# A gated long-convolution and linear-attention kernel rebuilt: FFT turns as matmuls, kernel tables made ahead, streams interleaved

## The chip, the cores and the metric

The kernel runs on one core of one Trainium2 chip. The metric is device time of one execution in microseconds (us); lower is better. Several executions are timed and the median is quoted.

## The reference

The output mixes two branches per row with a gate g. Branch `a` is a state-space convolution: for each of 512 channels a kernel K of 2048 taps is built from 128 complex exponentials, and u (2048 rows, 512 channels) is convolved with it through an FFT of length 4096. Branch `b` is linear attention with 32 heads of 16. The reference, cut to what matters:

```python
def reference(A_u, ..., B_wqkv, B_w_phi, B_wo, gate_w):
    # branch a
    logdA = dt * A                                         # complex, (512, 128)
    P = jnp.exp(logdA[:, :, None] * l[None, None, :])      # (512, 128, 2048)
    K = jnp.einsum("dn,dnl,dn->dl", Cc, P, dB).real        # (512, 2048)
    Kf, Uf = rfft(pad(K)), rfft(pad(u.T))                  # length 4096
    y = irfft(Uf * Kf)[:L].T + u * Dskip
    # branch b
    q, k, v = split(x @ wqkv)
    phi_q = concat(softmax(q w_phi), softmax(-q w_phi))    # phi_k alike
    o = (phi_q @ sum_s phi_k v) / (phi_q . sum_s phi_k + 1e-6)
    b = o @ wo
    # both
    g = sigmoid((x * gate_w).sum(-1))
    return g * y + (1 - g) * b                             # x = u
```

## The kernel before

Matmuls leave their results in PSUM, from where VectorE or ScalarE copies them out; such a copy is called an eviction here. The kernel runs phase after phase: loads and keys, queries and attention output, the FFT of u, and then four quarters of 128 channels, each with kernel generation, FFT of K, product, inverse FFT and output. An FFT step mixes rows within a partition block, and the next step needs another axis on the partitions. Before makes that turn by a trip through DRAM: SU for u, UHd for u's spectrum (written whole, read back by quarter), SK for K, SZ for the product.

```python
def kgen_chunk(nc, kp, c, cc, E_L, E_R, nE_R, psA, psK, wk, kst_sc):   # 32 channels
    ...                                                  # phase table of the left factor
    y = wk.tile([128, 32, 32], F32, name="k_y")
    nc.scalar.activation(out=y[:], in_=ps[:], func=ACT.Identity, bias=MAGIC)
    nc.vector.scalar_tensor_tensor(out=nf[:], in0=y[:], scalar=MAGIC, in1=ps[:], op0=ALU.subtract, op1=ALU.subtract)
    nc.scalar.activation(out=anf[:], in_=nf[:], func=ACT.Abs)
    nc.scalar.activation(out=msinL[:], in_=nf[:], func=ACT.Sin, scale=TWO_PI_S)
    nc.scalar.activation(out=cosL[:], in_=anf[:], func=ACT.Sin, scale=-TWO_PI_S, bias=HALF_PI)
    nc.vector.tensor_tensor(out=Lre[:], in0=E_L[:, dl0:dl0 + 32, :], in1=cosL[:], op=ALU.mult)
    nc.vector.tensor_tensor(out=mLim[:], in0=E_L[:, dl0:dl0 + 32, :], in1=msinL[:], op=ALU.mult)
    ...                                                  # right factor: Rre, Rim
    for pair in range(16):
        nc.tensor.matmul(o, lhsT=Rre[:, 2 * pair:2 * pair + 2, :], rhs=Lre[:, 2 * pair:2 * pair + 2, :], start=True, stop=False)
        nc.tensor.matmul(o, lhsT=Rim[:, 2 * pair:2 * pair + 2, :], rhs=mLim[:, 2 * pair:2 * pair + 2, :], start=False, stop=True)

def fft_stage_a(nc, fc, sc, kst_sc, SK, fp):
    ...                                                  # first step of K into Kt
    for ri in range(2):
        eng = nc.sync if ri == 0 else nc.scalar
        eng.dma_start(out=SK[ri, :, :, d0:d0 + 128].rearrange("q f d -> f q d"), in_=Kt[ri][:])
    st.MQ = fp.mq.tile([128, 32, 128], BF16, name="MQK")
    for ri in range(2):
        eng.dma_start(out=st.MQ[64 * ri:64 * ri + 64, :, :], in_=SK[ri, :, :, d0:d0 + 128].rearrange("q (fq f) d -> (q fq) f d", fq=4))

def fft_stage_b(nc, fc, st, Uh, SZ, fp):
    ...                                                  # second step, product: 8 x 6 DVE operations of 512
    for ro in range(2):
        eng.dma_start(out=SZ[ro, :, :, d0:d0 + 128].rearrange("q (fq f) d -> (q fq) f d", fq=4), in_=Zt[64 * ro:64 * ro + 64, :, :])
    for ro in range(2):
        eng.dma_start(out=st.ZT[ro][:], in_=SZ[ro, :, :, d0:d0 + 128].rearrange("q f d -> f q d"))

# full_kernel
BSd, gs = part_b(...)                                    # attention, whole
UHd = u_path_dram(nc, tc, fc, x2d, dram)                 # FFT of u, whole: SU, MQU, UHd
for qtr in range(5):
    ...                                                  # exp tables of the quarter
    for cc in range(4):
        if qtr < 4: kgen_chunk(...)
        if pending is not None:
            if cc == 0: ...; fft_stage_b(nc, fc, pending, Uh, SZ, fp)
            elif cc == 1: fft_stage_c(nc, fc, pending, fp, make_final(128 * pending.sc)); pending = None
    if qtr < 4: pending = fft_stage_a(nc, fc, qtr, kst_sc, SK, fp)
```

The softmax here doesn't subtract the row's maximum and nothing guards it: scores larger than these inputs give would overflow.

## Time and profile before

| | before |
|---|---|
| time, median of 3 runs | 647.84 us (643.49 to 651.64) |
| span of the profiled execution | 644.2 us |
| mean TensorE clock granted | 0.715 |
| instructions | 5205 |

The page cuts the span into 40 equal slices, here of 16.1 us. A digit is the busy share of an engine in that slice in tenths (9 is 90% or more); PE is TensorE, DVE VectorE, ACT ScalarE. PEclk is the TensorE clock in tenths, DMA the busy share of the 16 DMA engines. From the kernel before:

```profile
PE   0197738726755404655464654746536556452442
...
DVE  2399994397765503534725975449835399351932
ACT  0176529929533403568997534975448764441210
...
DMA  9800010400383885853015096160861707817035
...
DMA packets 150171, 61.20 MB, mean 95 GB/s; under 512 B 136704, under 2 KB 148224, under 8 KB 148992
```

Read the columns downwards. The fifteenth is the plainest: DMA 8, and 0 in all three rows above. In the second half, peaks of DMA return every few slices and no compute row holds an 8 or 9 for more than two slices: transfers and computing take turns. And 61.20 MB go in 150,171 packets, most under 512 bytes, while u and the output are 2 MB each. The groups, stages and chain that the argument starts from are in the prediction below.

### The profile page before, as it was taken

The page shows a single profiled execution, that of the slowest core. Times are in us where ns is not written, and L with a number is a line of the kernel's source. Part 1 is how long each engine was busy: PE and PEld are TensorE (multiplying, and loading weights), DVE is VectorE, ACT ScalarE, POOL GpSimd, SP SyncE. Part 2 cuts the span into 40 slices and gives each one's busy share as a digit, 9 for nine tenths or more (in the row PEclk, how much of TensorE's full clock was granted, in tenths as well). Part 3 has the DMA queues.
Part 4 walks back from the last instruction along what each step waited for, and adds up shares of the span by engine and source line. Part 5 has one row for each costly group of instructions (what it writes and reads, how often), then busy time and mean ns, then how long its engine had stood idle before and what let it go on. Part 6 is the DMA issues. An engine that isn't in the chain of part 4 may idle for free.

```text
span 644.2 us, 5205 instructions
## 1 busy us (share of the span) xinstructions
PE 334.6 (52%) x1600; PEld 127.8 (20%) x1600; DVE 384.0 (60%) x821; ACT 334.7 (52%) x477; POOL 49.7 (8%) x83
## 2 busy tenths in 40 slices
PE   0197738726755404655464654746536556452442
PEld 0143313201221101212231221312203121130010
DVE  2399994397765503534725975449835399351932
ACT  0176529929533403568997534975448764441210
POOL 9431000000360000000000000000000000000000
PEclk9999979959985856877676575765757766556565
DMA  9800010400383885853015096160861707817035
GB/s 156 163 1 2 1 11 0 127 4 1 112 249 104 236 228 162 243 247 66 1 44 87 1 184 128 49 98 1 158 137 38 126 0 128 163 37 130 0 66 113
DMA packets 150171, 61.20 MB, mean 95 GB/s; under 512 B 136704, under 2 KB 148224, under 8 KB 148992
## 3 DMA queue, kind: packets, MB, share of 16 engines
q1 hardware_dynamic: 77728, 29.52, 20.6%
q10 hardware_dynamic: 71264, 28.22, 20.4%
q0 software_dynamic: 1152, 3.15, 1.7%
q8 instruction: 12, 0.20, 0.1%
q14 instruction: 15, 0.12, 0.1%
HBM read 30.86 MB, written 26.87 MB: 90 GB/s over the span
## 4 chain that ended last, share of the span: by engine, by line
DMA 32%; DVE 31%; ACT 17%; PE 14%; issue 4%; ACTq 1%; DVEq 0%; SPq 0%
DMA SZ<-Zt 5%; DMA MQK<-SK 4%; DMA SU<-Ut 3%; DMA xT<-in_A_u_dram 3%; DVE Kre L422 3%; DMA UHd<-Uo 2%; DVE ot L744 2%; DMA MQU<-SU 2%; ACT E_R L209 2%; PE ups L674 2%; PE psP L391 2%; DVE phik L517 2%; DVE phik L519 1%; DVE k_y L222 1%; ACT k_anf L224 1%
## 5 line engine op out<-in xcount | busy, mean ns | idle before, releaser
L251 PE MATMUL kps<-k_Lre,k_Rre 128*128 128x64 bf16 x256 | 29.5, 238 | 33.1 <-DVE k_Lre L231 32.9
L676 DVE CAST Uo<-ups 128x512 bf16<-128x512 f32 x32 | 20.8, 687 | 40.9 <-PE ups L674 29.5
L423 ACT CAST Kim<-psQim 128x512 bf16<-128x512 f32 x32 | 18.5, 590 | 43.6 <-PE psQim L419 43.6
L678 ACT CAST Uo<-ups 128x512 bf16<-128x512 f32 x32 | 18.1, 587 | 43.6 <-PE ups L674 32.7
L418 PE MATMUL psQre<-MQK,BDQ_1649 128*128 128x512 bf16 x32 | 19.0, 594 | 32.0 <-DMA MQK<-SK 20.8
L251 PEld LDWEIGHTS <-k_Rre 128*128 128x128 bf16 x256 | 26.7, 128 | 37.9 <-DVE k_Lre L231 20.2
L209 ACT ACTIVATE E_R<-argps 128x1024 bf16<-128x1024 f32 x32 | 32.5, 1056 | 0.7 <-PE argps L206 0.6
L744 DVE SCALAR_TENSOR_TENSOR ot<-psY,gs,bs_in 128x128 bf16<-128x128 f32 x64 | 17.5, 342 | 25.0 <-PE psY L458 22.5
L422 DVE CAST Kre<-psQre 128x512 bf16<-128x512 f32 x32 | 21.8, 680 | 15.5 <-PE psQre L418 15.5
L206 PE MATMUL argps<-selR_110,statER 128*128 128x512 bf16 x64 | 22.4, 436 | 15.6 <-ACT E_L L201 12.7
L252 PE MATMUL kps<-k_mLim,k_Rim 128*128 128x64 bf16 x256 | 28.7, 239 | 2.3 <-DVE k_Rim L247 2.3
L252 PEld LDWEIGHTS <-k_Rim 128*128 128x128 bf16 x256 | 26.6, 128 | 15.7 <-issue 8.7
L232 DVE TENSOR_TENSOR k_mLim<-E_L,k_msinL 128x1024 bf16<-128x1024 bf16 x16 | 11.0, 689 | 31.1 <-ACT k_msinL L226 31.1
L210 DVE TENSOR_SCALAR nE_R<-E_R 128x4096 bf16<-128x4096 bf16 x4 | 4.9, 1227 | 40.0 <-ACT E_R L209 40.0
L419 PE MATMUL psQim<-MQK,BDQ_1650 128*128 128x512 bf16 x32 | 18.8, 589 | 17.3 <-DVE Kre L422 17.3
L627 PE MATMUL bps<-wo_sb,oT 128*128 128x512 bf16 x64 | 20.4, 465 | 12.6 <-ACT bs L629 11.7
L674 PE MATMUL ups<-MQU,BDQ_1649 128*128 128x512 bf16 x32 | 10.8, 462 | 30.1 <-DMA MQU<-SU 28.1
L629 ACT ACTIVATE bs<-bps,omg 128x512 bf16<-128x512 f32 x16 | 11.0, 687 | 23.7 <-DVE bs_1433 L633 4.4
L607 PE MATMUL aexp<-a_pm,Xst 128*128 128x512 bf16 x32 | 13.8, 443 | 17.1 <-DVE a_pm L599 14.7
L220 ACT ACTIVATE k_y<-argps 128x1024 f32<-128x1024 f32 x16 | 16.6, 1037 | 11.2 <-DVE ot L744 9.8
L443 ACT CAST Zt<-psZ 128x512 bf16<-128x512 f32 x16 | 9.4, 585 | 25.1 <-PE psZ L439 25.1
L224 ACT ACTIVATE k_anf<-k_y 128x1024 f32<-128x1024 f32 x16 | 16.8, 1052 | 8.9 <-DVE k_y L222 8.8
(792 smaller groups left out, 998.0 us busy)
## 6 DMA issues: line engine op xcount, KB each, us to landing
UHd<-Uo SPq DMA_DIRECT2D x4, 1024.0 KB, 4.3
UHd<-Uo ACTq DMA_DIRECT2D x4, 1024.0 KB, 4.3
bs_in<-BSd SPq DMA_DIRECT2D x16, 128.0 KB, 2.5
SU<-Ut SPq DMA_DIRECT2D x2, 1024.0 KB, 11.0
SU<-Ut ACTq DMA_DIRECT2D x2, 1024.0 KB, 9.6
MQU<-SU SPq DMA_DIRECT2D x1, 2048.0 KB, 12.7
MQU<-SU ACTq DMA_DIRECT2D x1, 2048.0 KB, 12.7
MQK<-SK SPq DMA_DIRECT2D x4, 512.0 KB, 6.9
```

The costliest lines, as they stand in the source:

```text
L206: nc.tensor.matmul(ps[:, 8 * j:8 * j + 8, :], lhsT=kp.statER[:, G, :], rhs=kp.selR64[:, d0:d0 + 8, :], start=True, stop=True)
L209: nc.scalar.activation(out=E_R[:, dd:dd + 16, :], in_=ps[:], func=ACT.Exp)
L224: nc.scalar.activation(out=anf[:], in_=nf[:], func=ACT.Abs)
L251: nc.tensor.matmul(o, lhsT=Rre[:, 2 * pair:2 * pair + 2, :], rhs=Lre[:, 2 * pair:2 * pair + 2, :], start=True, stop=False)
L252: nc.tensor.matmul(o, lhsT=Rim[:, 2 * pair:2 * pair + 2, :], rhs=mLim[:, 2 * pair:2 * pair + 2, :], start=False, stop=True)
L418: nc.tensor.matmul(psre[:], lhsT=fc.BDQ[0][:], rhs=MQ[:, fs, :], start=True, stop=True)
L419: nc.tensor.matmul(psim[:], lhsT=fc.BDQ[1][:], rhs=MQ[:, fs, :], start=True, stop=True)
L422: nc.vector.tensor_copy(out=Kre[:], in_=psre[:])
L627: nc.tensor.matmul(ps[:], lhsT=oT[:, m, 128 * st:128 * st + 128], rhs=wo_sb[:, m, :], start=(m == 0), stop=(m == 3))
L674: nc.tensor.matmul(ps[:], lhsT=fc.BDQ[ro][:], rhs=MQ[:, fp_, :], start=True, stop=True)
L676: nc.vector.tensor_copy(out=Uo[:, ff, :], in_=ps[:])
L744: nc.vector.scalar_tensor_tensor(out=ot[:, qq, :], in0=ps[:, qq, :], scalar=gs[:, q:q + 1], in1=bs[:, qq, :], op0=ALU.mult, op1=ALU.add)
```

## The change

The intent is to remove the turns, to have fewer and larger vector operations, and to let independent streams fill each other's gaps. Four parts:

1. **Turns of data become matmuls.** The data is the stationary operand (`lhsT`) and the FFT table the moving one, so that the product comes out turned. SU, SK and UHd go; one DRAM turn per quarter (Zd) stays, in halves. (The attention branch's output also still waits in DRAM until its quarter is put together, in `bSd`, as in before.)
2. **Kernel generation.** The left factor is a product of two small polar tables C and D, worked out once. Exponentials and sines of 64 channels are made one piece ahead of their use, with one switch of ScalarE's function table each way.
3. **Attention by blocks** of 256 (keys) and 512 rows (queries); the output projection is folded into `Mw`.
4. **Program order interleaves** the streams.

The diff cut to its core:

```diff
-def kgen_chunk(nc, kp, c, cc, E_L, E_R, nE_R, psA, psK, wk, kst_sc):
-    ...                                    # left phase table per chunk, see above
+def kgen_a(nc, C, D, wk, d0, n):
+    ...
+    for o, (i0, j0), (i1, j1), op in ((0, (0, 0), (1, 1), ALU.add), (1, (0, 1), (1, 0), ALU.subtract)):
+        nc.vector.tensor_tensor(out=A[:, o], in0=Cb(i0), in1=Db(j0), op=ALU.mult)
+        nc.vector.tensor_tensor(out=tmp[:], in0=Cb(i1), in1=Db(j1), op=ALU.mult)
+        nc.vector.tensor_tensor(out=A[:, o], in0=A[:, o], in1=tmp[:], op=op)
+def kgen_chunk(nc, kps, A, R):
+    for e in range(2):
+        for g4 in range(4):
+            for ri in range(2):
+                for dj in range(4):
+                    d = 16 * e + 4 * dj + g4
+                    nc.tensor.matmul(kps[32 * dj:32 * dj + 32, g4, e, :], lhsT=A[:, ri, :, :, d].rearrange("p a b -> p (a b)"),
+                                     rhs=R[:, ri, d, :], start=(ri == 0), stop=(ri == 1), tile_position=(0, 32 * dj), skip_group_check=True)
...
-        eng.dma_start(out=SK[ri, :, :, d0:d0 + 128].rearrange("q f d -> f q d"), in_=Kt[ri][:])
-        eng.dma_start(out=st.MQ[64 * ri:64 * ri + 64, :, :], in_=SK[...])
+def fft_stage_a(nc, fc, ps_pool, lhs, XA_dst, ev):
+    ...
+            nc.tensor.matmul(ps[:, i, :], lhsT=l[0], rhs=rhs, start=True, stop=True)     # data stationary
+    ev(XA_dst, ps[:].rearrange("p g (x d) -> p x d g", d=4))
...
-        for b in range(8): ...             # 6 products and sums of 512, Kre and Kim apart
+        nc.vector.tensor_tensor(out=t12[:], in0=Us, in1=XK[:], op=ALU.mult)
+        nc.vector.tensor_tensor(out=t34[:], in0=Us, in1=XK[:, :, ::-1, :], op=ALU.mult)
+        ...                                # the sums are made in PSUM by the inverse's matmuls
+            nc.sync.dma_start(out=Zd[:, :, rs, :].rearrange("i t r d -> (i t) r d"), in_=Z[:, rs, :])
+            ...
+                    nc.sync.dma_start(out=ZT[p0:p0 + step, :, :], in_=Zd[ri, 32 * th:32 * th + 32, rs, :].rearrange("t r d -> r t d"))
...
-    BSd, gs = part_b(...)
-    UHd = u_path_dram(nc, tc, fc, x2d, dram)
-    for qtr in range(5): ...
+    polar = compute_polar(nc, act, persist, tp, ring, rawd, ld_b, ident)
+    C, D = next(polar)
+    act.begin(TRIG)
+    next(polar, None)
+    ...
+    fold_projection(nc, at, wraw, 512, wT, Wkp, ident, ring, evu)
+    u_path(nc, fc, UD, xau, XU, ring, evu, 2)
+    ...                                    # keys, fold
+    query(0)
+    tabs[1] = kgen_tables(1)
+    Eq[2] = query_exp(nc, act, qp, psA, xT, Wqp, 2)
+    query(1)
+    kgen(0)
+    ...
+    fft(0)
+    for Q in range(1, 4):
+        for h in (2 * Q, 2 * Q + 1):
+            if h + 1 < 8:
+                tabs[h + 1] = kgen_tables(h + 1)
+            kgen(h)
+        fft(Q)
+        finish(Q - 1)
+    finish(3)
```

## The prediction

> **What bounds the kernel now.** I read the page's busy shares first, then the windows by stage, the chain of waits, and the costs by group.
>
> ```profile
> PE 334.6 (52%) x1600; PEld 127.8 (20%) x1600; DVE 384.0 (60%) x821; ACT 334.7 (52%) x477; POOL 49.7 (8%) x83
> ```
>
> No engine is full: the busiest, VectorE (DVE), works 384.0 of 644.2 us. The loss is in the gaps, so I cut the span where the program changes stage (columns: stretch, length, then busy time of PE, PEld, DVE, ACT and POOL, TensorE clock, DMA share, GB/s).
>
> ```profile
> 0.00:83.00 83.00, 43.34 (x364) 23.21 (x365) 60.08 (x164) 33.51 (x62) 32.64 (x59) 1.00 0.37 63
> 83.00:205.00 122.00, 72.96 (x244) 24.55 (x244) 84.50 (x172) 71.14 (x120) 17.11 (x24) 0.81 0.27 78
> 205.00:283.00 78.00, 33.38 (x96) 10.89 (x95) 32.79 (x51) 27.80 (x49) 0.00 (x0) 0.69 0.73 218
> 283.00:341.00 58.00, 32.31 (x206) 14.72 (x207) 24.06 (x33) 52.08 (x59) 0.00 (x0) 0.76 0.25 64
> 341.00:423.00 82.00, 46.38 (x224) 17.75 (x224) 51.39 (x109) 50.82 (x62) 0.00 (x0) 0.63 0.49 90
> ...
> 587.00:645.00 58.00, 19.96 (x40) 4.29 (x40) 28.14 (x76) 7.03 (x12) 0.00 (x0) 0.53 0.37 64
> ```
>
> Loads and attention keys take 0 to 83, queries and attention output 83 to 205, the FFT of u 205 to 283, then four quarters of 128 channels, 82 us apart, and a tail of 58 us. In the FFT of u no compute engine is half busy and DMA has 73%: it goes through DRAM twice. In a repeated quarter DVE works 51 of 82 us. The chain of waits says what the rest is:
>
> ```profile
> DMA 32%; DVE 31%; ACT 17%; PE 14%; issue 4%; ACTq 1%; DVEq 0%; SPq 0%
> ```
>
> A third of the end-setting chain (206 us) is transfers. In its time order the second quarter shows them naked:
>
> ```profile
> 422.82 6.45 DMA MQK<-SK
> ...
> 462.81 9.74 DMA SZ<-Zt
> 472.58 4.29 DMA ZT_3516<-SZ
> ```
>
> With the 2.69 us of SK<-Kt ahead of them, 23 us per quarter. So the bound is **latency**: phases in order, four DRAM turns inside them, TensorE half cold in between.
>
> **What the Trainium skill says.** (1) "TensorE: Matmul & The Clock Gate", Part 1: the array runs at half clock until it has been busy for about 3.4 us. Agrees: the clock is 1.00 up to 83 us and 0.53 in the tail; 64-column matmuls follow each other every 53 ns in the timeline near 304 us, 512-column ones every 216 ns near 37 us and 430 ns near 98 us. (2) "VectorE: DVE Perf Modes", tier table: two-source operations do two bf16 elements a cycle from SBUF and one from PSUM. Agrees: k_mLim, 1024 bf16 elements, 689 ns; the PSUM cast Kre, 512 elements, 680 ns. (3) "TensorEngine Tiling (Array Packing)", Key Properties: small tiles work in parallel, but changing the tiling mode drains the engine. No trace here shows either: the one tiled group of before (the query sums) has its tiles 216 ns apart, one after another. (4) "ScalarE: Activation LUTs", What ACT_TABLE_LOAD costs: 1283 ns for the load. Agrees: every load of the trace takes 1283 ns.
>
> **The change, part by part.** I use five durations of before: DVE two-source bf16, 1024 elements, 0.69 us; DVE with a PSUM or f32 source, 512 elements 0.69 and 1024 elements 1.22 (k_y, 1212 ns); ACT 512 elements 0.59, 1024 elements 1.04; small operations 0.2 to 0.4.
>
> ```profile
> L222 DVE SCALAR_TENSOR_TENSOR k_y<-k_y,argps 128x1024 f32<-128x1024 f32 x16 | 19.4, 1212 | 0.4 <-ACT k_y L220 0.4
> L232 DVE TENSOR_TENSOR k_mLim<-E_L,k_msinL 128x1024 bf16<-128x1024 bf16 x16 | 11.0, 689 | 31.1 <-ACT k_msinL L226 31.1
> L422 DVE CAST Kre<-psQre 128x512 bf16<-128x512 f32 x32 | 21.8, 680 | 15.5 <-PE psQre L418 15.5
> L423 ACT CAST Kim<-psQim 128x512 bf16<-128x512 f32 x32 | 18.5, 590 | 43.6 <-PE psQim L419 43.6
> L209 ACT ACTIVATE E_R<-argps 128x1024 bf16<-128x1024 f32 x32 | 32.5, 1056 | 0.7 <-PE argps L206 0.6
> ```
>
> *Kernel generation.* The left phase table per chunk (k_y, k_anf, k_msinL, k_cosL, E_L on ACT; k_y, k_Lre, k_mLim on DVE) goes; its values come from products of two small tables, C and D. DVE per 32 channels: 6 + 4 two-source operations of 1024 and one negation: 10 x 0.69 + 0.42 = 7.3; sixteen times: 117 us. ACT per 64 channels: 4 exponentials + 4 sines x 1.04 + 2 table loads 2.6 + 3 evictions 3.1 = 14; eight times: 112 us.
>
> *FFT of K, inverse, output.* Turns of data become matmuls with the data stationary; SK is gone, one DRAM turn (Zd, in halves) stays. Per quarter DVE: 8 products x 0.69 + 2 output products x 1.22 = 8 us, where before it had 6 x 8 x 0.42 + 8 x 0.68 + 4 x 0.69 + 16 x 0.34 = 34. ACT: 8 evictions x 1.04 = 8. Four quarters: DVE 34 with two evictions of the last, ACT 31.
>
> *FFT of u.* Both DRAM turns go (SU<-Ut, MQU<-SU, UHd<-Uo, about 50 us of the chain), and the stage becomes 32 evictions, plus 8 of the folded projections: ACT 27 x 1.02 = 28, DVE 13 x 1.22 = 16.
>
> *Attention.* Keys: per 256 rows DVE 2 reductions x 1.22 + 4 x 0.69 = 5.2, ACT 3.0; eight times 42 and 24. Folding 4 and 6. Queries: per 512 rows DVE 8 x 0.69 + 1.5 = 7.0, ACT 8 x 0.6 + 1.5 + 4 x 0.59 = 8.7; four times 28 and 35. The output projection is folded into Mw, so oT with its evictions goes, and the long reciprocals (3.3 us each) go to exp and ln on ACT.
>
> *Set-up.* FFT constants, selectors, masks: DVE 23, ACT 5. Rates and polar tables C, D: DVE 40, ACT 27 (16 f32 passes of 512 and four trigonometric blocks of 1024). Turning x, gates, table loads: ACT 13.
>
> *Sums.* DVE 117 + 34 + 16 + 42 + 4 + 28 + 23 + 40 = 304, against 384. ACT 112 + 31 + 28 + 24 + 6 + 35 + 5 + 27 + 13 = 281, against 335. PE issues about 4,700 matmuls against 1,600, most small. By columns: 448 of 512, 448 of 256, 1,632 of 128, 2,176 of 64 or fewer. At the paces above (216, 108, 54 and 30 ns warm, the last two estimated from the first and from 27 ns between 1-column matmuls near 24 us) that is 97 + 48 + 88 + 65 = 298 us one after another and warm, about 560 cold (430, 215, 107, 53). Parallel tiles would save up to a quarter; I take **340**, my least certain number.
>
> *From sums to a span.* Three engines now have near 300 each, so no stage can be shorter than its busiest engine; I go through the stages. Loads, constants, rates: u is 2 MB in 256-byte pieces; before moved such pieces at 1 MB in about 6.5 us (MQK), so 14 us behind the first loads; DVE has 27 us: 30. Polar tables with turning x, the FFT of u and the folds beside them: ACT 62, DVE 53, with ping-pong between them: 65, to 95. Keys: before, DVE ran them gaplessly at 2.9 us per 128 rows; now 2.6 of work but longer chains: 50, to 145. Fold: 8. Queries with the first two kernel pieces beside them: DVE 57, ACT 63, PE 90 to 110: 85, to 238. Three quarters of kernel and FFT, DVE 37, ACT 36, PE 28 warm and 48 cold in each, sharing two PSUM slots for tables and kernel blocks: 43 each, to 367. Tail of the last quarter: FFT and inverse 17, two DRAM legs at 4 to 6 us partly behind it 7, output 12: about 36. Together **403**.
>
> **The rivals.**
> - *TensorE becomes the bound.* For it: three times the instructions, weights read at strides (the A slices and the turned u), mode changes that drain, a clock that falls in gaps (0.63 in the repeated quarters). Against: 340 of 403 is hidden if the streams do mix. If tiles don't overlap and it stays cold: 480 to 520.
> - *PSUM slots and single buffers replace the DRAM wait.* R, Atmp and KD have one buffer and a kernel block holds one of two slots for two chunks, about 9 of 15 us. If each quarter serializes to 60, the time is 403 + 3 x 17 = 455.
> - *The streams mix perfectly.* DVE at 85% would give 304 / 0.85 = 358. For it: before ran DVE without a gap from 40 to 80 us when its inputs were there.
> - *The removed turns were hidden anyway.* Against: they lie naked on the chain. Only Zd stays, and it has the next quarter's kernel to hide behind, except in the last.
>
> **Range and chances.** The centre is the stage sum, 403; the mixing rival sets the low end, 345, the PSUM and part of the TensorE rival the high end, 475. Even the worst I can build, 520, is 20% below 647.84 us, so "slower" has only what I can't see: faster 0.97, same 0.01, slower 0.02.
>
> **What would show it.** DVE busy 290 to 320 and ACT 265 to 300 confirm the sums; PE busy above 400 or a mean clock below 0.65 makes TensorE the failed term. The DMA share of the chain should fall from 32% to under 12%, most of it in the first 20 us and the last 20. The kernel products of 1024 must take near 0.69 us although one operand is repeated; at 1.22 DVE would gain 96 x 0.53 = 51 us and the time about 45. The repeated quarter should be near 43 us. If PE waits most for PSUM slots to be emptied, the second rival is right.

## The result, and the profile after

| | before | after |
|---|---|---|
| time, median of 4 | 646.13 us (643.49 to 651.64) | 411.48 us (410.56 to 412.68) |
| ratio, with its 95% interval | | 0.6363 (0.6327 to 0.6400) |
| span profiled | 644.2 us | 410.5 us |
| VectorE, ScalarE, TensorE busy | 384.0, 334.7, 334.6 us | 274.2, 257.2, 271.4 us |
| mean clock | 0.715 | 0.763 |
| moved by DMA | 61.20 MB | 21.54 MB |

The output is correct.

The page of the kernel after, the busy line, the slices (now of 10.3 us) and the chain:

```profile
PE 271.4 (66%) x4712; PEld 164.5 (40%) x4712; DVE 274.2 (67%) x470; ACT 257.2 (63%) x335; POOL 7.2 (2%) x19
...
PE   0465100397997877879997999764876778767621
...
DVE  8956667644477847943874379697959695925502
ACT  3589452888565494786549726979695979643000
...
PEclk9985555589699989688999899886588656665555
DMA  9991000000000000000010011255000950045894
...
ACT 34%; PE 28%; DVE 24%; DMA 6%; issue 4%; SPq 2%; DVEq 0%; ACTq 0%
```

DMA has nearly gone from the end-setting chain (6% where before had 32%), and from the fifth slice to the twenty-fifth its row shows 0 or 1. Three engines share the chain, none full. Two holes are left: the fifth to seventh slices, where PE shows 1, 0, 0, and the last three, where ScalarE shows 0.

The windows of the trace after, cut where the program changes stage (same columns as in the prediction):

```profile
0.00:27.00 27.00, 9.36 (x151) 8.52 (x152) 21.25 (x62) 15.90 (x18) 7.18 (x19) 1.00 1.09 186
27.00:76.00 49.00, 7.81 (x68) 6.56 (x67) 33.46 (x63) 28.53 (x37) 0.00 (x0) 0.51 0.10 25
76.00:103.00 27.00, 21.25 (x569) 19.35 (x569) 14.49 (x14) 21.63 (x24) 0.00 (x0) 0.81 0.01 2
103.00:158.00 55.00, 47.12 (x607) 18.92 (x607) 36.33 (x48) 35.28 (x62) 0.00 (x0) 0.91 0.01 2
158.00:170.00 12.00, 7.95 (x106) 3.35 (x106) 10.79 (x26) 4.68 (x11) 0.00 (x0) 0.78 0.00 0
170.00:254.00 84.00, 77.81 (x802) 40.00 (x800) 55.36 (x100) 54.68 (x90) 0.00 (x0) 0.93 0.07 25
254.00:367.00 113.00, 79.32 (x1906) 52.37 (x1905) 88.11 (x146) 90.54 (x92) 0.00 (x0) 0.71 0.33 69
367.00:411.00 44.00, 20.74 (x520) 15.43 (x519) 14.43 (x16) 5.91 (x7) 0.00 (x0) 0.50 0.73 121
```

They are set-up, polar tables, FFT of u, keys, fold, queries with the first kernel pieces, the repeated quarters, and the tail. Between 254 and 367 us VectorE and ScalarE work 78% and 80% of the time; that is where mixing pays. In the tail ScalarE works 5.91 of 44 us.

The first hole, in the timeline (start, length, instruction, in brackets the idle time before it and what ended it), and the second, from the chain's order of time:

```profile
34.39 2.83 PE L381 MATMUL psA<-W,UD 128*64 128x256 bf16 x24
...
40.35 0.99 ACT L70 CAST Wkp<-wps 128x1024 bf16<-128x1024 f32 x1
...
43.69 1.28 ACT L91 ACT_TABLE_LOAD   x1
...
77.15 3.81 PE L381 MATMUL psA<-W,UD 128*64 128x256 bf16 x32 [34.64 <-ACT XAu L70]
```

```profile
386.67 4.49 DMA Zd<-Z
...
394.19 6.79 DMA ZT<-Zd
```

UD, u as it was loaded, was there early: the same operation had done 24 matmuls from 34.39 us on and 8 more at 41.39, which fill the four PSUM slots that it has. Then PE idled 34.6 us, until the first evictions into XAu, which ran only after the polar tables' sines. Order alone is a poor explanation: in the program text the folded key projection stands behind the sines too, and its evictions ran ahead of them (Wkp at 40.35, the sines' table load at 43.69). What sets XAu apart is that the program gives it its memory only where the tables' scratch has been freed. So the wait looks like one for memory; experiment 6 comes back to it. At the end the last quarter's turn lies open: 4.49 us out, 3 us until the loads of ZT had been issued one after the other, 6.79 us until the last landed.

The groups of the after page that answer to the durations used in the prediction (busy us, mean ns of one, then the idle time before them):

```profile
L96 ACT ACTIVATE E<-args 128x1024 bf16<-128x1024 f32 x32 | 31.3, 1034 | 2.9 <-PE args L313 2.9
...
L91 ACT ACT_TABLE_LOAD x20 | 25.7, 1283 | 1.1 <-PEq L917 0.7
L341 DVE TENSOR_TENSOR A<-Ctab,Dtab 128x1024 bf16<-128x1024 bf16 x32 | 21.6, 690 | 6.6 <-PE kps L368 6.6
...
L368 PE MATMUL kps<-R,A 128*32 128x64 bf16 x1024 | 19.8, 234 | 5.1 <-ACT cs L96 3.5
```

The kernel products take 690 ns although one operand is repeated. The 1,024 kernel matmuls last 234 ns each, 240 us if laid end to end, but keep PE busy for 19.8 us: they overlap.

### The profile page after: what moved, and what is told of

Same layout as the page of the kernel before. It is cut to its first block, busy times and chain, and to the rows that moved or that the text cites. A ratio compares the mean times of both kernels' runs of the same rounds, so it can differ in the third digit from the quotient of the medians.

```text
span 410.5 us, 10580 instructions
## 1 busy us (share of the span) xinstructions
PE 271.4 (66%) x4712; PEld 164.5 (40%) x4712; DVE 274.2 (67%) x470; ACT 257.2 (63%) x335; POOL 7.2 (2%) x19
## 2 busy tenths in 40 slices
DMA packets 56317, 21.54 MB, mean 52 GB/s; under 512 B 52048, under 2 KB 54736, under 8 KB 56272
## 4 chain that ended last, share of the span: by engine, by line
ACT 34%; PE 28%; DVE 24%; DMA 6%; issue 4%; SPq 2%; DVEq 0%; ACTq 0%
PE bps L680 6%; ACT E L96 5%; ACT cs L96 4%; ACT L91 3%; PE pk L576 3%; ACT Eq L96 3%; DMA UD<-in_A_u_dram 3%; PE psz L444 3%; ACT XK L70 2%; PE psB L402 2%; DVE vr L591 2%; DVE Eq L676 2%; ACT Ek L96 2%; ACT xT L70 2%; ACT Z L70 2%
## 5 line engine op out<-in xcount | busy, mean ns | idle before, releaser
L444 PE MATMUL psz<-t,TI 64*128 64x128 bf16 x512 | 28.7, 277 | 16.2 <-DVE t L435 12.6
L444 PEld LDWEIGHTS <-TI 64*128 64x128 bf16 x512 | 23.5, 124 | 28.0 <-issue 22.8
L680 PE MATMUL bps<-Mw,Eq 128*128 128x512 bf16 x128 | 33.6, 410 | 1.4 <-DVE Eq L676 1.1
L96 ACT ACTIVATE E<-args 128x1024 bf16<-128x1024 f32 x32 | 31.3, 1034 | 2.9 <-PE args L313 2.9
L96 ACT ACTIVATE cs<-args 128x1024 bf16<-128x1024 f32 x32 | 30.7, 1037 | 0.1
L402 PEld LDWEIGHTS <-TB 64*64 64x64 bf16 x1152 | 23.0, 136 | 11.0 <-issue 6.8
L91 ACT ACT_TABLE_LOAD x20 | 25.7, 1283 | 1.1 <-PEq L917 0.7
L341 DVE TENSOR_TENSOR A<-Ctab,Dtab 128x1024 bf16<-128x1024 bf16 x32 | 21.6, 690 | 6.6 <-PE kps L368 6.6
L313 PE MATMUL args<-selE,stat 64*128 64x512 bf16 x64 | 22.0, 448 | 4.8 <-ACT E L96 2.7
L368 PE MATMUL kps<-R,A 128*32 128x64 bf16 x1024 | 19.8, 234 | 5.1 <-ACT cs L96 3.5
L342 DVE TENSOR_TENSOR Atmp<-Ctab,Dtab 128x1024 bf16<-128x1024 bf16 x32 | 22.1, 691 | 0.3
L343 DVE TENSOR_TENSOR A<-A,Atmp 128x1024 bf16<-128x1024 bf16 x32 | 22.1, 690 | 0.1
L368 PEld LDWEIGHTS <-A 128*32 128x32 bf16 x1024 | 17.7, 151 | 10.3 <-issue 9.1
```

The lines of the kernel that those rows point to most:

```text
L91: p = self.nc.scalar.preload_act_table_set(name)
L96: i = self.nc.scalar.activation(**kw)
L342: nc.vector.tensor_tensor(out=tmp[:], in0=Cb(i1), in1=Db(j1), op=ALU.mult)
L343: nc.vector.tensor_tensor(out=A[:, o], in0=A[:, o], in1=tmp[:], op=op)
L368: nc.tensor.matmul(kps[32 * dj:32 * dj + 32, g4, e, :], lhsT=A[:, ri, :, :, d].rearrange("p a b -> p (a b)"), rhs=R[:, ri, d, :], start=(r ...
L402: nc.tensor.matmul(o, lhsT=fc.TB[rows, r, op, :], rhs=rhs, start=(op == 0), stop=(op == 2), tile_position=(64 * e, 64 * rpar), skip_group_ ...
```

## The experiments

Theory: the 235 us come from (a) the DRAM turns that lay on the chain, (b) mixing by placement, (c) less work. Rivals: the turns were hidden anyway; the order in the program is worth little; a new bound (TensorE, PSUM slots) holds the after kernel. Kernels went to three chips, each with its own runs of before (medians 645.7 to 649.4 us). So a cost against after is worked out below as (ratio of the variant − 0.6363) × 646.1 us. Each ratio has an interval of about ±0.0035, which makes such a difference uncertain by about 3 us. Figures inside a run are from its one profiled execution.

### 1. Before without the turns of K and of the product

Wrong on purpose (relative error 0.092): the next step reads what the last one left, unturned, with the same number and sizes of matmuls and evictions.

```diff
-    for ri in range(2):
-        eng.dma_start(out=SK[...], in_=Kt[ri][:])
-    st.MQ = fp.mq.tile([128, 32, 128], BF16, name="MQK")
-    for ri in range(2):
-        eng.dma_start(out=st.MQ[...], in_=SK[...])
+    st.MQ = Kt
...
-    for ro in range(2): eng.dma_start(out=SZ[...], in_=Zt[...])
-    for ro in range(2): eng.dma_start(out=st.ZT[ro][:], in_=SZ[...])
+    st.ZT = [Zt[:, 0:16, :], Zt[:, 16:32, :]]
```

> The kernel before, without the two DRAM turns of each quarter (SK written and read as MQK, SZ written and read as ZT): the next matmuls read the tiles that were to be sent, so the result is wrong on purpose; all engine work is as it was. Theory (the turns lay naked on the path, 23 us per quarter in the chain of waits): 646 - 4 x 21 = 560 us, 545 to 580. Rival (they were hidden, or another wait takes their place): above 620 us.

Measured: 569.77 us against 649.42, ratio 0.8788 (0.8744 to 0.8832), so 80 us less. The turns were on the end-setting path, 20 us a quarter; the rival that they were hidden falls.

### 2. Before without the turn of u as well

Wrong on purpose too (0.077). The first step of u writes MQU directly; UHd stays, since it holds the spectrum between stages.

```diff
+        MQ = up.tile([128, 32, 512], BF16, name="MQU")
...
-                Ut = uw.tile([128, 8, 512], BF16, name="Ut")
+                Ut = MQ[:, 8 * (2 * ri + h):8 * (2 * ri + h) + 8, :]
...
-                eng.dma_start(out=SU[...], in_=Ut[:])
-        for ri in range(2):
-            eng.dma_start(out=MQ[...], in_=SU[...])
```

> As b_no_k_turns, and the turn of u between its two FFT stages (SU written, read as MQU; 35 us of the chain) is gone too; UHd is still written and read. Wrong result on purpose. Theory: 35 us less than b_no_k_turns, so about 525 us, 505 to 545; then turns explain about 120 of the 235 us gained and the rest is less work and better mixing. Rival (nearly all of the gain is removed turns): 420 to 460 us.

Measured: 539.67 us, ratio 0.8306 (0.8258 to 0.8355): 110 us less than before in all, 30 for SU. The busy line of this kernel:

```profile
PE 319.7 (59%) x1600; PEld 125.4 (23%) x1600; DVE 383.9 (71%) x821; ACT 333.1 (62%) x477; POOL 49.8 (9%) x83
```

The work of VectorE is what it was (384.0 us); what went is gaps, and some TensorE time: PE is busy 319.7 us instead of 334.6, at a mean clock of 0.793 instead of 0.715. So the turns, with the higher clock that came with their removal, are 110 of the 235 us, less than half. What UHd's trip cost was not measured.

### 3. After with a DRAM turn put back

One trip of XA through DRAM per quarter, ahead of its use, on SyncE's queue as all of after's transfers. The result stays right.

```diff
+        def turn(Q):
+            Xd = dram.tile([32, 128, nd], BF16, name=f"Xd{Q}")
+            ...
+                nc.sync.dma_start(out=Xd[rs].rearrange("r p x -> p r x"), in_=XA[:, rs].rearrange("p r i c -> p r (i c)"))
+            ...
+                nc.sync.dma_start(out=XA[:, rs].rearrange("p r i c -> p r (i c)"), in_=Xd[rs].rearrange("r p x -> p r x"))
+
         def fft(Q):
+            turn(Q)
```

> The kernel after, with a DRAM turn given back: XA, 1 MB per quarter, is written to DRAM in 256-byte pieces and read back into the same tile before the second FFT stage, as before did with SK; the result stays right. The turn alone takes 11 to 14 us by the times of before. Theory (the mixed streams hide a turn when another quarter's kernel lies beside it; only the last quarter has nothing beside it): 10 to 25 us longer. Rival (a turn lies naked whatever is beside it): 4 x 12, about 48 us longer.

Measured: 451.91 us, ratio 0.6968 (0.6936 to 0.7000), +39 us. The theory that a mixed program hides most of a turn missed with its 10 to 25; the rival's 48 is too high. The chain in its last part:

```profile
389.50 4.73 DMA Zd<-Z
...
397.79 6.74 DMA ZT<-Zd
404.55 3.32 DMA Xd<-XA
...
407.93 4.18 DMA XA<-Xd
```

The groups of KD's eviction from 240 us on (seven of eight; first and last start) tell when the kernel of the last quarter was there; first after, then this kernel:

```profile
L70 ACT CAST KD<-kps x7: 1012/1012/1032, 247.3 to 363.0; 128x1024 bf16<-128x1024 f32 x7
```

```profile
L70 ACT CAST KD<-kps x7: 1012/1012/1017, 245.8 to 369.4; 128x1024 bf16<-128x1024 f32 x7
```

So the earlier turns delayed the last kernel piece by only 6.4 us: they were nearly hidden. In the last quarter the next matmul group of the FFT began at 412.16 us, 42.8 us after that eviction, where after needs 4.1 (367.09 on its chain). Of these 42.8 us the two transfers take 7.5; XA was complete at about 374.9 (its last eviction), but until 404.55 the turn stood in the queue behind the Zd and ZT transfers and the outputs of the quarter before. (6.4 and 42.8 − 4.1 make 45, not 39: some 6 us came back afterwards, for from that matmul group to the end are 37.6 us, in after 43.4.) That made a new theory: the cost is mostly the queue.

### 4. The same turn on GpSimd's queue

```diff
-                nc.sync.dma_start(out=Xd[rs]...
+                nc.gpsimd.dma_start(out=Xd[rs]...
-                nc.sync.dma_start(out=XA[:, rs]...
+                nc.gpsimd.dma_start(out=XA[:, rs]...
```

> As a_turn (a DRAM turn of XA given back in each quarter), but its transfers are issued from GpSimd's queue, which does nothing else, instead of SyncE's queue, where in a_turn they stood in line behind the transfers of ZT and the outputs (the last turn was issued at 404 us, its data had been there since about 345). Theory (a transfer is hidden if its issue isn't blocked; only the last turn, 11 to 14 us, is naked): 12 to 22 us longer than the kernel after. Rival (the FFT that follows the turn in the program order holds the engines, whatever the queue): 35 to 45 us longer, as a_turn's 40.

Measured: 429.46 us against 645.67, ratio 0.6643 (0.6603 to 0.6683), +18 us. PE's timeline of this kernel at the last quarter, and KD's eviction:

```profile
387.19 1.92 PE L402 MATMUL psB<-XA,TB 64*64 64x128 bf16 x96 [12.09 <-DMA XA<-Xd]
```

```profile
L70 ACT CAST KD<-kps x7: 1012/1012/1019, 247.6 to 366.6; 128x1024 bf16<-128x1024 f32 x7
```

Now the gap in the last quarter is 20.6 us, and the theory's 12 to 22 holds. (The expectation's "since about 345" was a misreading: in experiment 3 the last kernel eviction is at 369.4.) The same bytes, in their own queue, cost 21 us less: that much of the 39 was waiting in order behind other transfers. One thing more changed with the queue: the page lists GpSimd's as `software_dynamic`, SyncE's as `hardware_dynamic`; what that alone does was not tested. Of the remaining 18, the last turn takes 14.0, from the first issue at 373.15 to 387.15 on the chain, in the one quarter that has nothing left to hide it; the last kernel eviction comes 3.6 us later than in after.

### 5. After with its placement undone

Same instructions; queries first, tables directly before their use, each quarter finished before the next starts.

```diff
         query(0)
-        tabs[1] = kgen_tables(1)
         Eq[2] = query_exp(nc, act, qp, psA, xT, Wqp, 2)
         query(1)
-        kgen(0)
...
-        tabs[2] = kgen_tables(2)
+        kgen(0)
+        tabs[1] = kgen_tables(1)
         kgen(1)
...
         fft(0)
+        finish(0)
...
-                if h + 1 < 8:
-                    tabs[h + 1] = kgen_tables(h + 1)
+                tabs[h] = kgen_tables(h)
                 kgen(h)
             fft(Q)
-            finish(Q - 1)
-        finish(3)
+            finish(Q)
```

> The kernel after, same instructions, program order undone: all query blocks first, then the kernel pieces; the tables of each piece right before it instead of one piece ahead; finish of a quarter right after its FFT instead of one quarter later. Theory (the placement makes the mixing): 25 to 60 us longer. Rival (instructions are mixed at build time whatever the order of the text, so placement is worth little): within 8 us.

Measured: 454.40 us, ratio 0.7009 (0.6971 to 0.7048), +42 us, as the theory expected. The same stretch of time as after's seventh (here the repeated quarters start at about the same time but last longer, so it holds fewer of their instructions):

```profile
254.00:367.00 113.00, 66.48 (x1372) 39.48 (x1366) 73.59 (x122) 74.08 (x74) 0.00 (x0) 0.61 0.26 53
```

VectorE works 73.6 of the 113 us instead of 88.1, ScalarE 74.1 instead of 90.5, and the clock falls from 0.71 to 0.61. Busy time in all is unchanged (275.3 and 258.5 us). Like for like: from the last kernel eviction of the first quarter to that of the last (KD at 245.8 and 388.6) are 142.8 us, in after 115.7, so 27 us of the cost lie in the quarters; from there to the end are 62.0 instead of 47.5. Order in the program is a real part of the gain, not decoration.

### 6. The FFT of u ahead of the polar tables' sines

This goes for the first hole. XAu gets space of its own, in four pieces, and a scratch pool gives up one of nine buffers.

```diff
+        xau = pool(cu, "xau")
+        evu = Evict(nc, "aav")
         C, D = next(polar)
+        fold_projection(nc, at, wraw, 512, wT, Wkp, ident, ring, evu)
+        u_path(nc, fc, UD, xau, XU, ring, evu, 4)
         act.begin(TRIG)
         next(polar, None)
...
-        fold_projection(nc, at, wraw, 512, wT, Wkp, ident, ring, evu)
-        u_path(nc, fc, UD, xau, XU, ring, evu, 2)
```

> The kernel after with one part moved: the folded key projection and the FFT of u are put ahead of the trigonometric half of the polar tables, with a buffer XAu of their own (four pieces of 8 KB per partition instead of two of 16 KB; one scratch buffer fewer for the tables). In the kernel after TensorE waits 34.6 us at 42 us for the first eviction of XAu while ScalarE and VectorE are only 55 to 62% busy with the tables. Theory (that wait is a wait for memory, and the two stages can share the engines): 12 to 25 us shorter, about 392 us. Rival (the tables' chain of dependences is only made longer by the evictions between its links): within 4 us of the kernel after.

Measured: 398.83 us, ratio 0.6176 (0.6154 to 0.6199), −12 us, at the small end of what was expected. The same window as after's second:

```profile
27.00:76.00 49.00, 25.45 (x735) 23.01 (x736) 35.83 (x59) 37.38 (x47) 0.00 (x0) 0.69 0.12 27
```

PE has 25.45 us of work where it had 7.81, and ScalarE 37.4 where it had 28.5. So the two stages can share the engines. The edit changes place and memory together, so it doesn't separate them. That the wait of 34.6 us gave only 12 is plausible, not shown: in the wait (42 to 76 us) ScalarE and VectorE were already busy for 48% and 65%, and the FFT's evictions are theirs.

### 7. The last quarter's loads and stores on two queues

```diff
-                    nc.sync.dma_start(out=ZT[p0:p0 + step, :, :], ...
+                    (nc.sync if ri == 0 or q2 is None or r0 == 0 else q2).dma_start(out=ZT[p0:p0 + step, :, :], ...
...
-                nc.sync.dma_start(out=ov[c, :, j0:j0 + nj, :], ...
+                (nc.sync if c % 2 == 0 or q2 is None else q2).dma_start(out=ov[c, :, j0:j0 + nj, :], ...
```

Here `q2` is ScalarE's queue for the last quarter, and not given for the others.

> The kernel after, half of the last ZT loads and of the last output stores issued from ScalarE's queue, which is idle by then. Theory (the issue of 8 loads takes 4.5 us and of 8 stores as long on one queue, after the last Zd has landed): 2 to 5 us shorter. Rival (the landing, not the issue, sets the end): within 1 us.

Measured: 407.80 us, ratio 0.6302 (0.6271 to 0.6333), −4 us. It lies in the expected range, but the interval overlaps after's (0.6327 to 0.6400), so it is not settled.

### 8. 32 VectorE operations more

```diff
         nc.vector.tensor_tensor(out=tmp[:], in0=Cb(i1), in1=Db(j1), op=ALU.mult)
+        nc.vector.tensor_tensor(out=tmp[:], in0=Cb(i1), in1=Db(j1), op=ALU.mult)
```

> The kernel after with one product of each kernel table computed twice (32 more VectorE operations of 1024 bf16 elements, 32 x 0.60 = 19 us of work; the result stays right). If VectorE were the bound of the kernel stage: 19 us longer. Theory (three engines near balance, none full): about half of it, 7 to 14 us longer. If VectorE has room: under 3 us.

Measured: 415.76 us, ratio 0.6428 (0.6397 to 0.6460), +4 us for 21.6 us of VectorE work (busy 295.8 us). That is between the theory and the rival, and clear of neither. Where the cost lies is shown with experiment 9.

### 9. 16 ScalarE sines more

```diff
     act(out=cs[:, 1], in_=ps[:], func=ACT.Sin, scale=TWO_PI)
+    act(out=cs[:, 1], in_=ps[:], func=ACT.Sin, scale=TWO_PI)
```

> The kernel after with the sine table of each kernel piece computed twice (16 more ScalarE operations of 1024 elements, 16 x 0.94 = 15 us of work; result right). Theory (ScalarE, which the chain of waits names most, 34%, is the engine nearest to a bound in the kernel stage): 8 to 15 us longer, where twice-computed VectorE work of 19 us cost 4. Rival (no engine binds, all have room): under 5 us.

Measured: 422.60 us against 646.80, ratio 0.6524 (0.6486 to 0.6562), +10 us for 15.2 us of work (busy 272.4 us). Over the whole span two thirds of what ScalarE gets more shows in the time, against a fifth for VectorE. It is tempting to call ScalarE the nearest to a bound. The traces don't bear that out for the repeated quarters. Here the span is cut at two of KD's evictions, the last of the first quarter and the last of the fourth:

| run | up to the first cut, us | between the cuts, us | behind the second, us | work added between the cuts |
|---|---|---|---|---|
| after | 247.3 | 115.7 | 47.5 | |
| 8: VectorE products | 245.4 | 124.0 | 46.0 | 16.1 us of VectorE |
| 9: ScalarE sines | 252.3 | 121.8 | 46.5 | 9.1 us of ScalarE |

In the quarters the added products cost 8.3 us (half of their work) and the sines 6.2 (two thirds). The two runs differ ahead of the quarters, where the sines cost 5.0 us and the products nothing. These are single executions, and the executions of one run agree within about 1%, so 0.52 and 0.68 are not clear of each other. Work added to either engine shows in good part there, so neither stands out as the bound.

### 10. The kernel matmuls one column tile after another

The same 1,024 matmuls and tiles; only the nesting of the loops changes, so that neighbours in the stream use the same tile.

```diff
-    for e in range(2):
-        for g4 in range(4):
-            for ri in range(2):
-                for dj in range(4):
+    for dj in range(4):
+        for e in range(2):
+            for g4 in range(4):
+                for ri in range(2):
```

> The kernel after, same 1,024 kernel matmuls of 128x32 weights by 64 columns, only their order changed: all of one column tile, then the next, instead of the four tiles in turn. In the kernel after 128 of them take about 2.1 us, 16 ns each. Theory (that pace is four tiles at work together; one tile alone goes at 27 to 53 ns as in the kernel before): their busy time rises from 20 to between 35 and 55 us, and the whole by 5 to 25 us. Rival (small weights alone make the pace, not the tiles): no change, within 3 us.

Measured: 424.29 us, ratio 0.6565 (0.6529 to 0.6601), +13 us. The group in this kernel:

```profile
L368 PE MATMUL kps<-R,A 128*32 128x64 bf16 x1024 | 52.7, 229 | 5.1 <-ACT cs L96 3.5 <-DVE R L357 1.2 <-ACT XA L70 0.3
```

PE is busy with it for 52.7 us instead of 19.8, while one matmul lasts as long as before. In time order, 128 of them took 6.0 us instead of 2.06, so 47 ns from start to start instead of 16. Alternating the tiles is worth 33 us of TensorE in this group and 13 us of time. PE's busy time in all rose by only 12 us (283.5), since the mean clock was higher here (0.825 against 0.763). Cut as in experiment 9, the quarters take 124.7 us, 9.0 more for 15.1 us more of TensorE: much the same share again. The new order also puts the two matmuls that add up in one place next to each other. That is not the reason for the pace: in the trace the second matmul of such a pair follows the first no later than the next pair follows (mostly 56 or 57 ns, in some stretches 25 to 33). In after four starts, one per tile, lie within some 10 ns, and then mostly 43 to 56 ns pass.

### 11. One PSUM slot for the FFT instead of two

```diff
-        psF = pool(ctx, "psF", 2, space=PSUM)
+        psF = pool(ctx, "psF", 1, space=PSUM)
```

> The kernel after with one PSUM slot instead of two for the FFT stages (psF). Rival of the prediction (PSUM slots are the bound): over 25 us longer. Theory (slots are not short, the bound is engines and their chains): under 12 us longer.

Measured: 420.47 us, ratio 0.6498 (0.6462 to 0.6535), +9 us. The FFT's two slots are used, but halving them costs little, within the theory's 12. It is a narrow test of the prediction's second rival, which meant the slots that tables and kernel blocks share (`psP` in the program) and the single buffers of R, Atmp and KD; those were not varied. What answers that rival is the measured quarter, 40 to 42 us where it has 60, below.

### 12. Experiments 6 and 7 together

> Both gains together: the FFT of u ahead of the trigonometric tables (a_u_first, 12.7 us shorter) and the last transfers on two queues (a_tail, 3.7 us shorter). They lie in different stages, so the sum should hold: 395 us, 392 to 398. If they overlap: 399.

Measured: 398.19 us, ratio 0.6155 (0.6129 to 0.6181), correct: −13 us against after, and faster than both kernels. But it is no faster than experiment 6 alone (0.6176) within the intervals: the gains did not add. The end of its chain:

```profile
376.43 4.48 DMA Zd<-Z
...
381.05 4.72 DMA ZT<-Zd
...
386.15 3.00 DMA out_dram<-ot
```

From the start of Z's store to ZT's landing it now takes 9.3 us, where after takes 14.3 and experiment 6, by its own chain, 14.1 (373.64 to 387.71). But Z's store starts 2.8 us later than in experiment 6 (376.43 against 373.64), and the output stores on the chain take 3.00 us where it had 1.95. So most of what the loads save is given back ahead of Z's store and in the output stores. Of the 2.8 us, 2.2 are there already at the last kernel eviction (KD at 352.2, in experiment 6 at 350.0), ahead of every transfer that was changed; why was not tested.

## Why the prediction was right

The time, 411 us, is 2% above the predicted 403, within 345 to 475. Point by point:

**The bound before, latency in phases with the turns naked: right, and measured.** "They lie naked on the chain" said the prediction of the turns: removing SK and SZ gave 80 us and SU another 30, the higher clock included.

**"Only Zd stays, and it has the next quarter's kernel to hide behind, except in the last": right for this kernel, for a narrower reason than it sounds.** Experiment 3 shows that a turn is not hidden because other work exists; a turn also needs a queue in which nothing stands ahead of it, and the last quarter has no cover at all.

**The stages.** The prediction's own stage ends against the windows:

| stage | predicted length (end), us | measured length (end), us |
|---|---|---|
| set-up | 30 (30) | 27 (27) |
| polar, FFT of u | 65 (95) | 76 (103) |
| keys | 50 (145) | 55 (158) |
| fold | 8 (153) | 12 (170) |
| queries, first kernel pieces | 85 (238) | 84 (254) |
| three quarters | 129 (367) | 113 (367) |
| tail | 36 (403) | 44 (411) |

The sum is right partly because errors cancel. Up to 254 us the kernel is 16 us late, and the stretch of the three quarters takes it back. From the last kernel eviction of one quarter to that of the next (KD at 247.3, 287.1, 328.9 and 363.0 us) it is 39.8, 41.8 and 34.1 us, where the prediction took 43 for each. The middle one, with 33.4 us of VectorE, 33.7 of ScalarE and 30.1 of TensorE in it, is the repeated quarter that was meant, and it was read well. The last is shorter: by the program it prepares no tables for a next quarter, which the prediction did not count. So it is in part luck that the whole came within 2%.

**The step that failed: "the FFT of u and the folds beside them".** Only the fold of the keys and the first 32 matmuls of the FFT ran beside the polar tables; the rest ran after them, with PE idle for 34.6 us. The stage took 76 us, not 65. Experiment 6 makes the step true by place and memory, and gains 12 us.

**The tail, 36, was 44.** The prediction took "two DRAM legs at 4 to 6 us partly behind it 7"; in the chain they take 4.49, 3 (issue) and 6.79 us, with nothing beside them.

**The sums were too high.** VectorE 304 against 274, ScalarE 281 against 257: outside the 290 to 320 and the 265 to 300 that were named. The durations and counts were right (690 ns against 0.69 us, 1034 against 1.04), but multiplying count by duration counts an overlap twice. In VectorE's timeline, operations of 0.69 us begin every 0.60 us (299.51, 300.11), in ScalarE's those of 1.02 us every 0.90 (254.80, 255.71, 256.60). Added up over all instructions of the trace of after, durations come to 308.7 us on VectorE and 282.5 on ScalarE, within 2% of the prediction's 304 and 281; the busy times are less by the overlaps, 34.4 and 25.3 us. For the same reason "304, against 384" compares two kinds of figure: 384 is a busy time, and the durations of before add up to 445. The Trainium skill has it for ScalarE, in "ScalarE: Activation LUTs", What ACT_TABLE_LOAD costs: back-to-back operations overlap by about 93 ns. The prediction read that section for the table load and missed this. A better estimate takes starts, not durations, from the timeline.

**TensorE, 340, was 271.** The mis-sized term is "parallel tiles would save up to a quarter". For the one group that experiment 10 measures, alternating tiles cut the busy time from 52.7 to 19.8 us, by 62%; the other tiled groups were not measured apart. (The "about 560 cold" is 579 by the paces it lists.) That TensorE would not be the bound was right: after has it busy 66%, at a mean clock of 0.763.

**"The streams mix perfectly", 358: not over the span.** VectorE reached 67%, not 85%. In the three quarters it comes close: 94.8 of the 115.7 us between the KD evictions, 82%. What is missing lies outside them, most of all in the FFT of u (14.49 of 27 us, 54%) and the tail (14.43 of 44 us, 33%).

**"PSUM slots and single buffers", 455: no.** A quarter takes 40 to 42 us, not 60. In 254 to 367 us PE waits longest for the products `t` (12.6 us); its waits for a slot of the tables to be emptied come to 9.0.

**The clock.** The prediction gives 1.00 up to 83 us as agreement. The view does show that, but the matmuls of 128 columns that start at 30.94 us follow one another every 107 ns, the slow pace, and those of 512 columns start 430 ns apart at 34.31 and 34.74, but 216 from 35.08 on. So the view's 1.00 can't be taken for the first 35 us; the two paces, and the change after some 4 us of matmuls, do agree with the page. The second agreement has a wrong example too: Kre is a one-source cast.

**Where the 235 us come from.** 110 are the DRAM turns, by experiments 1 and 2. Placement is worth 42 in the new kernel, by experiment 5. The remaining some 83 would be less work in fewer instructions on VectorE and ScalarE (110 and 77 us of busy time less) and UHd; that is the difference that remains, argued and not shown, and the parts need not add exactly, since the first is measured in before and the second in after.

## What to carry to other kernels

Read a chain's naked transfers as time that can be had, but ask where each stream will stand in the program and in its DMA queue: here order alone was worth 42 us and a shared queue 21. Estimate sums from start to start, not from durations. Look for a bound by adding work to an engine, and see in which stage the cost arises before naming the engine: over the span ScalarE looked nearest here, in the repeated quarters none of the three stood out. A stage in which two streams should run side by side is a claim to be checked in the timeline before it goes into a sum.

## What the Trainium skill lacked or had wrong

- "ScalarE: Activation LUTs", What ACT_TABLE_LOAD costs, has 1283 ns for the load and about 2.66 us for a switch. The load agrees. The switch doesn't: one operation ends at 258.57, the load runs from 258.59 for 1.28 us and the next operation begins at 259.88, so 1.31 us from end to start. So it is for 17 of the 19 loads of after that stand between two operations (the other two: 1.73 and 2.13).
- "TensorE: Matmul & The Clock Gate", Part 1, says that start-to-start never drops below about 25 ns. For matmuls on four column tiles in turn it is 16 ns on average here (128 in 2.06 us), and in one tile 47 (experiment 10); the sentence needs the words "in one tile", as the page's own Part 3, on tiles, implies.
- "DMA: Bandwidth & Descriptors", Issuing engines are not separate DMA queues, says that issuing from several engines saves only the time to initiate a transfer. Here the same transfers cost 21 us less on a queue of their own (experiments 3 and 4; the kind of queue changed too): in the shared queue they stood behind transfers that weren't ready. The page lacks that a queue shared by streams of different readiness is a dependency between them.
